# Sums for the first token pair of the second expert layer: temporaries in the row buffers instead of the relu buffers

## The chip, the cores and the metric

The kernel runs on one core of a Trainium2 chip. The metric is device microseconds of one execution. Before the change the median of 3 runs is 716.48 us (714.12 to 718.5).

## What is computed

Causal attention with a bias from a cumulated gate, then a layer in which each of 1152 tokens goes to one of 8 experts, then a layer in which each token goes through all 4 experts with weights of its own:

```python
attn_out = _attn_ref(**attn_kwargs)                      # B, H, S, D = 2, 8, 576, 64
x = attn_out.transpose(0, 2, 1, 3).reshape(B * S, H * D) # 1152 x 512
x = _moe_ref(x=x, **moe_kwargs)    # out[mask] = gate_w * (relu(x[mask] @ w1[e]) @ w2[e]), one of 8
return _moe2_ref(x=x, **moe2_kwargs)  # out += p[:, e] * (relu(x @ w1[e]) @ w2[e]), all 4; F = 1024
```

## The kernel before

**Attention** and the routing come first; the change is behind them.

**The first expert layer** runs over 8 slots, one expert each, with fixed capacities `CAPS` (128 to 248 columns; slot 7 has 188). For a slot, `fetch` starts the loads of the gathered rows (`xw`, pool `mp`, tag "xw", two buffers of 128 x 2 x 512 f32) and of the weights, `turn_x` (L728 to L733) transposes the rows on TensorE into `xs`, `layer1` (L777 to L784) multiplies by the first weight in eight groups `f` = 0 to 7 into PSUM tiles `pg` (three buffers) and evicts each through relu into `hb`, even groups by ScalarE (L784), odd ones by VectorE (L782). `layer2` (L804) multiplies `hb` by the second weight in four column blocks `dc`, and `put_y` (L790, L792) evicts them into `xf`. The tile `hb` has the tag "hh" and a single buffer, so a slot's `hb` may be written only when the tile that had the buffer before is read for the last time. The tag "hl" belongs to a lower part that only the split slot (248 columns) has. The transposes of slot 7's rows stand ahead of slot 6's `layer2`.

**Between slots 6 and 7** the program calls `build(0, ...)`: it prepares the moving operands of the second layer for the first pair of token blocks (2 x 288 columns of `xf`). The second layer multiplies 2 x 2 blocks with seven products in place of eight, so `build` makes four sums of blocks (`tsum`, two tiles of 128 x 2 x 2 x 288 f32, each with two sums; L648 on VectorE), and for every block and sum a rounded high part (`xbh`, `xth`; ScalarE, L645 and L649) and a low part (`xbl`, `xtl`; VectorE, L646 and L650). Its sums 1 and 3 are formed from sum 0, sum 1 in the first temporary and sum 3 in the second. The two temporaries take tiles of the tags named in the call.

**Beside it** the first weights of the second layer are prepared: four sums (`wsum`, L865 to L868) and, by `finish_first`, high parts (`hi`, ScalarE L872) and low parts (`wl`, VectorE L873) of 128 x 1024. The two weight tiles of `second_half` are loaded (L656) when buffers of the pool `wp` come free, and summed by GpSimd (L903). Slot 7's own weights are loaded ahead of these.

**After slot 7** stands `tc.If(most > 0)` (L914), a branch that handles tokens above the capacities; no instruction of its body runs with these inputs. All engines pass through the branch. Then the second layer starts with `first_layer` (L958) and keeps TensorE busy to the end.

A scheduler orders each engine's instructions from this program text, buffers and estimated times, so that the rows of one engine can be in another order than the calls.

Of the kernel before, what the change touches and what calls it, by code (L numbers as in the profile page):

```python
# [381 lines left out]
def tile_attention_moe_moe(  # L382
# [210 lines left out]
    mp = top1.enter_context(tc.tile_pool(name="mp", bufs=1))  # L593
# [38 lines left out]
    def build(c, pool, tags, bufs=1):  # L632

        o = 2 * HT * c
        blk = lambda j, k: xf[:, 2 * j : 2 * j + 2, o + k * HT : o + (k + 1) * HT]
        if ops[c] is None:
            ops[c] = [(pool if c else xo).tile([P, n, 2, HT], F32R, name=f"x{w}{c}") for w, n in (("bh", 3), ("bl", 3), ("th", 4), ("tl", 4))]
        bh, bl, th, tl = ops[c]
        t = [pool.tile([P, 2, 2, HT], F32, tag=tag, name="tsum", bufs=bufs) for tag in tags]
        base = (blk(0, 0), blk(1, 0), blk(1, 1))  # L640
        one, two = t[0][:, 0], t[0][:, 1]
        sums = ((0, one, blk(0, 1), blk(0, 0)), (2, t[1][:, 0], blk(1, 1), blk(0, 1)), (1, two, blk(1, 1), one), (3, t[1][:, 1], blk(1, 0), two))
        for i in range(4):
            if i < 3:
                nc.scalar.activation(out=bh[:, i], in_=base[i], func=AF.Copy)  # L645
                nc.vector.tensor_tensor(out=bl[:, i], in0=base[i], in1=bh[:, i].bitcast(F32), op=ALU.subtract)  # L646
            j, o_, x, y = sums[i]
            nc.vector.tensor_tensor(out=o_, in0=x, in1=y, op=ALU.subtract)  # L648
            nc.scalar.activation(out=th[:, j], in_=o_, func=AF.Copy)  # L649
            nc.vector.tensor_tensor(out=tl[:, j], in0=o_, in1=th[:, j].bitcast(F32), op=ALU.subtract)  # L650
# [22 lines left out]
    def reg(ap, engines, hi):  # L673
        return nc.values_load(ap, engines=engines, min_val=0, max_val=hi, skip_runtime_bounds_check_because="by construction")
# [43 lines left out]
    def turn_x(xw, cap, split):  # L718

        xs = mp.tile([P, KC, 256], F32R if split else F32, tag="xs", name="xs", bufs=2)  # L720
        xsl = mp.tile([P, KC, 256], F32R, tag="xs", name="xsl", bufs=2) if split else None
        for j in range(2):
            pt = ps.tile([P, 2, 256], F32, tag="tp", name="tp")
            for jj in range(2):
                for i in range(-(-cap // P)):
                    w = min(P, cap - i * P)
                    cc = 2 * j + jj
                    nc.tensor.transpose(out=pt[:, jj, i * P : i * P + w], in_=xw[:w, i, cc * P : (cc + 1) * P], identity=ident[:w, :w])  # L728
            o = xs[:, 2 * j : 2 * j + 2, :cap]
            if j == 0 or split:  # L730
                nc.scalar.activation(out=o, in_=pt[:, :, :cap], func=AF.Copy)
            else:
                nc.vector.tensor_copy(out=o, in_=pt[:, :, :cap])  # L733
            if split:
                nc.vector.tensor_tensor(out=xsl[:, 2 * j : 2 * j + 2, :cap], in0=pt[:, :, :cap], in1=o.bitcast(F32), op=ALU.subtract)
        return xs, xsl
# [23 lines left out]
    def layer1(pa, xs, cap, load=None):  # L760
        xs, xsl = xs
        split = xsl is not None
        hb = mp.tile([P, FC, max(CAPS)], F32R if split else F32, tag="hh", name="hb")
        hbl = mp.tile([P, FC, max(CAPS)], F32R, tag="hl", name="hbl") if split else None
        marks[2] = hb
        for f in range(FC):
            if load and f % 2 == 0:
                load(f // 2)
            pg = ps.tile([P, 512], F32, tag="g1", name="pg", bufs=3)
            fs = slice((f % 2) * P, (f % 2) * P + P)  # L770
            w = pa[f // 2]
            pairs = ((w[0], xs), (w[0], xsl), (w[1], xs)) if split else ((w, xs),)
            n = len(pairs) * KC
            for i in range(n):
                wt, xt = pairs[i % len(pairs)]
                cc = i // len(pairs)
                nc.tensor.matmul(out=pg[:, :cap], lhsT=wt[:, cc, fs], rhs=xt[:, cc, :cap], start=i == 0, stop=i == n - 1)  # L777
            if split:
                nc.scalar.activation(out=hb[:, f, :cap], in_=pg[:, :cap], func=AF.Relu)
                marks[0] = nc.vector.scalar_tensor_tensor(out=hbl[:, f, :cap], in0=pg[:, :cap], scalar=0.0, in1=hb[:, f, :cap].bitcast(F32), op0=ALU.max, op1=ALU.subtract)  # L780
            elif f % 2:
                marks[0] = nc.vector.tensor_scalar(out=hb[:, f, :cap], in0=pg[:, :cap], scalar1=0.0, scalar2=None, op0=ALU.max)  # L782
            else:
                nc.scalar.activation(out=hb[:, f, :cap], in_=pg[:, :cap], func=AF.Relu)  # L784
        return hb, hbl
# [23 lines left out]
    def fetch(sl):  # L809
        ev = reg(meta[0:1, 0, sl : sl + 1] if sl else e0[0:1, :], (ET.SP,), E1 - 1)  # L810
        rows = lambda a, w: region[ds(ev, 1), a : a + w, :].rearrange("o n d -> (o n) d")
        xw = [load_x(rows, CAPS[sl])] if sl else []
        first = None if sl else lambda: xw.append(load_x(rows, CAPS[sl]))
        pa, pb = load_w(w1[ds(ev, 1)].rearrange("o k f -> (o k) f"), w2[ds(ev, 1)].rearrange("o k f -> (o k) f"), SPLIT[sl], first, True)
        if sl == 0:
            put_rows(L0, L0 + LATE)
        return pa, pb, xw[0]

    r0 = reg(e0[0:1, :], (ET.SP,), E1 - 1)
    pa, pb, xw = fetch(0)  # L820
# [13 lines left out]
    def later(pb, j):  # L834
        if j >= 2:
            with tc.issue_after(marks[0].ins):
                pb[j] = split_w(pb[j], home(4 + j))
# [6 lines left out]
    for sl in range(E1):  # L844
        last = sl == E1 - 1
        hs = layer1(pa, xs, CAPS[sl], rest if sl == 0 else (lambda j: later(pb, j)) if SPLIT[sl] else None)
        if sl == 0:
            with tc.issue_after(marks[0].ins):
                gates()
        if not last:  # L850
            na, nb_, xw = fetch(sl + 1)
            xs = turn_x(xw, CAPS[sl + 1], SPLIT[sl + 1])
        if sl == 1:
            most = reg(meta[0:1, 4, 0:1], everyone, N)
        off = reg(meta[0:1, 2, sl : sl + 1], (ET.Activation, ET.DVE), N if sl > 3 else sl * N // E1)
        layer2(pb, hs, off, CAPS[sl])
        if not last:
            pa, pb = na, nb_
        if sl == E1 - 2:

            build(0, mp, ("hl", "hh"))

    def four_sums(g, a, eng):

# [49 lines left out]
    with tc.If(most > 0):  # L914
        with tc.For_i(0, E1, 1) as sl:
            ev = reg(meta[0:1, 0, ds(sl, 1)], (ET.SP,), E1 - 1)
            cnt_r = reg(meta[0:1, 1, ds(sl, 1)], (ET.SP, ET.Activation, ET.DVE), N)
            off_r = reg(meta[0:1, 2, ds(sl, 1)], (ET.Activation, ET.DVE), N)
            ov_r = reg(meta[0:1, 3, ds(sl, 1)], everyone, N)
            with tc.For_i(0, ov_r, P) as i:  # L920
                within = lambda x, hi: nc.s_assert_within(x, 0, hi, skip_runtime_bounds_check_because="i < count - capacity")
                r0 = within(cnt_r - P - i, N - P)
                ox = load_x(lambda a, w: region[ds(ev, 1), ds(r0, w), :].rearrange("o n d -> (o n) d"), P)
                xt = turn_x(ox, P, False)
                wt = mp.tile([P, 3, 4 * 256], F32, tag="hl", name="wt")
                part = lambda j, c: wt[:, j % 3, :].rearrange("p (c f) -> p c f", c=c)
                ht = layer1([part(j, KC) for j in range(4)], xt, P, lambda j: load_a(part(j, KC), w1[ds(ev, 1)].rearrange("o k f -> (o k) f"), j))
                oo = within(off_r + cnt_r - P - i, N - P)
                for dc in range(KC):
                    py = ps.tile([P, 512], F32, tag="g2", name="py", bufs=3)  # L930
                    wc = wt[:, dc % 3, :].rearrange("p (c d) -> p c d", c=FC)
                    nc.sync.dma_start(out=wc, in_=w2[ds(ev, 1), :, dc * P : (dc + 1) * P].rearrange("o (c p) d -> p (o c) d", p=P))
                    for f in range(FC):
                        nc.tensor.matmul(out=py[:, :P], lhsT=wc[:, f, :], rhs=ht[0][:, f, :P], start=f == 0, stop=f == FC - 1)
                    put_y(dc, py[:, :P], oo, P)
        build(0, mp, ("hl", "hh"))
    top1.close()


# [176 lines left out]
```

## Time and profile before

| | |
|---|---|
| runs | 714.12, 716.48, 718.5 us |
| profiled execution | 723.46 us, of it the span 721.8 us |
| mean granted TensorE clock, share of full speed | 0.971 |
| busy | TensorE 95%, VectorE 62%, ScalarE 46%, GpSimd 23% |

All durations below come from the profiled execution, which is 7.0 us above the median of the runs. An engine's instructions run in order; what stands in brackets behind a row of the timeline is the idle time of that engine ahead of the row, and what ended it. A share of busy time is a mean over stages with different limits, so the stage around the change is read by itself, by its time line, its waits and its clock.

### The profile page before, as it was taken

To read this page: it belongs to the slowest core of one execution; us is meant where nothing else is said; L and a number is where in the kernel's file an instruction comes from. 1 tells how busy PE (TensorE), PEld (TensorE's weight loads), DVE (VectorE), ACT (ScalarE), POOL (GpSimd) and SP (SyncE) were. 2 spreads that over 40 slices of the span, in tenths; PEclk is the share of its full clock that TensorE was granted. 3 is DMA by queue.
4 is the path that set the end of the run, shared out by engine and by line. 5 is a ranking of instruction groups with operands and counts; after the bars stand their busy time and mean duration, and the time that the engine had idled before them with its cause. 6 is when DMAs were issued, how large, how long until landed. Compare 5 with 4: busy or idle time off the path is not lost.

```text
span 721.8 us, 12757 instructions
## 1 busy us (share of the span) xinstructions
PE 688.4 (95%) x4829; PEld 638.9 (89%) x4830; DVE 444.4 (62%) x1006; ACT 332.3 (46%) x617; POOL 167.6 (23%) x193
## 2 busy tenths in 40 slices
PE   7899999979899999968999999999999999999996
PEld 5799999868799999968999989989899899998995
DVE  7586867662017111453787775877869668777583
ACT  5576767521116111332652836636437265383541
POOL 2000000033300000001053423632336124332333
PEclk9899999979899999989999999999999999999998
DMA  6746666029986977310011110111011101211002
GB/s 139 190 111 181 156 178 176 1 109 340 364 273 208 330 245 233 113 59 3 1 60 59 59 56 5 59 59 45 16 57 59 59 1 59 60 59 39 21 30 102
DMA packets 87015, 78.92 MB, mean 109 GB/s; under 512 B 42699, under 2 KB 67275, under 8 KB 86951
## 3 DMA queue, kind: packets, MB, share of 16 engines
q1 hardware_dynamic: 83063, 72.76, 33.2%
q0 software_dynamic: 1776, 4.79, 1.8%
q10 hardware_dynamic: 2112, 0.52, 0.4%
q8 instruction: 39, 0.64, 0.4%
q14 instruction: 25, 0.20, 0.1%
HBM read 69.08 MB, written 8.99 MB: 108 GB/s over the span
## 4 chain that ended last, share of the span: by engine, by line
PE 49%; issue 1%; DVE 1%; ACT 1%; POOL 0%; POOLq 0%
PE py L1049 15%; PE qa L958 14%; PE qd L958 7%; PE qa L1036 6%; PE qb L958 4%; PE qd L1036 3%; PE qb L1036 1%; DVE acc L1009 1%; ACT hr L981 0%; POOL out_dram L403 0%; ACT hi L872 0%; POOLq L1111 0%; ACT hr L975 0%; DVE sl L873 0%; POOLq L403 0%
## 5 line engine op out<-in xcount | busy, mean ns | idle before, releaser
L975 ACT ACTIVATE hr<-qa 128x288 f32<-128x288 f32 x96 | 37.3, 407 | 93.5 <-PE qa L958 93.5
L903 POOL TENSOR_TENSOR wsum<-w 128x512 f32<-128x512 f32 x16 | 24.3, 1532 | 238.6 <-PE pg L777 128.7
L777 PE MATMUL pg<-xs,w 128*128 128x128 f32 (+6 forms) x448 | 66.9, 313 | 9.4 <-ACT hb L784 6.1
L777 PEld LDWEIGHTS pg<-xs,w 128*128 128x128 f32 x448 | 65.3, 205 | 10.5 <-ACT hb L784 6.4
L872 ACT ACTIVATE bh<-hr 128x512 fp32r<-128x512 f32 (+1 forms) x72 | 41.1, 584 | 62.8 <-PE py L1049 57.5
L1049 PE MATMUL py<-hi,bl 128*128 128x512 f32 x160 | 63.0, 394 | 0.0
L1049 PE MATMUL py<-hi,bh 128*128 128x512 f32 x160 | 63.0, 394 | 0.0
L1049 PE MATMUL py<-wl,bh 128*128 128x512 f32 x160 | 63.0, 394 | 0.0
L804 PE MATMUL py<-hb,w 128*128 128x128 f32 (+6 forms) x448 | 61.9, 296 | 0.7 <-DMA w<-in_moe_w_dram 0.7
L804 PEld LDWEIGHTS py<-hb,w 128*128 128x128 f32 x448 | 59.5, 190 | 1.5 <-DMA w<-in_moe_w_dram 1.1
L873 DVE TENSOR_TENSOR bl<-hr,bh 128x512 fp32r<-128x512 f32 (+1 forms) x72 | 55.5, 779 | 3.1 <-ACT bh L872 2.8
L283 PE MATMUL av<-vt,ptT 128*128 128x65 f32 x320 | 47.1, 279 | 0.0
L873 DVE TENSOR_TENSOR wl<-w,hi 128x1024 fp32r<-128x1024 f32 x32 | 45.4, 1420 | 0.0
L258 ACT ACTIVATE p<-p,mn 128x512 f32<-128x512 f32 (+4 forms) x72 | 40.6, 582 | 10.1 <-DVE mn L246 9.5
L1009 DVE SCALAR_TENSOR_TENSOR acc<-py,aux,acc 128x512 f32<-128x512 f32 x35 | 26.3, 751 | 28.4 <-PE py L1049 28.4
L271 ACT ACTIVATE ptT<-pt 128x512 f32<-128x512 f32 (+3 forms) x80 | 34.3, 434 | 19.3 <-PE pt L269 19.0
L283 PEld LDWEIGHTS av<-vt,ptT 128*128 128x128 f32 x320 | 42.5, 197 | 0.3
L958 PE MATMUL qa<-xbh,hi 128*128 128x288 f32 x128 | 39.6, 309 | 2.7 <-DVEq L914 2.6
L872 ACT ACTIVATE hi<-wsum 128x1024 fp32r<-128x1024 f32 x32 | 33.0, 1057 | 16.1 <-POOL wsum L868 13.3
L873 DVE TENSOR_TENSOR wl<-wsum,hi 128x1024 fp32r<-128x1024 f32 x32 | 38.9, 1216 | 0.0
L246 DVE CUSTOM_DVE_ANT_0 p<-sc,p 128x512 f32<-128x512 f32 (+4 forms) x72 | 34.6, 484 | 7.0 <-PE sc L209 4.3
L782 DVE TENSOR_SCALAR hb<-pg 128x128 f32<-128x128 f32 (+6 forms) x28 | 8.9, 317 | 48.5 <-PE pg L777 48.4
(297 smaller groups left out, 2044.8 us busy)
## 6 DMA issues: line engine op xcount, KB each, us to landing
w<-in_moe_w_dram SPq DMA_DIRECT2D x96, 512.0 KB
region<-zrow SPq DMA_DIRECT2D x8, 512.0 KB
bc<-ncum_d SPq DMA_DIRECT2D x7, 576.0 KB
ks<-in_k_dram SPq DMA_DIRECT2D x28, 128.0 KB
br<-ncum_d SPq DMA_DIRECT2D x16, 144.0 KB
qs<-in_q_dram SPq DMA_DIRECT2D x16, 128.0 KB
vt<-in_v_dram SPq DMA_DIRECT2D x16, 128.0 KB
xw<-region SPq DMA_DIRECT2D x8, 256.0 KB
```

The source lines that it names most:

```text
L246: self.last[1] = nc.vector.tensor_tensor_reduce(out=t[:, lo : lo + w], in0=st["sc"][:, 0:w], in1=t[:, lo : lo + w], scale=1.0, scalar=init ...
L258: self.last[0] = nc.scalar.activation(out=t[:, 0:w], in_=t[:, 0:w], func=AF.Exp, scale=-1.0, bias=st["mn"][:, 0:1])
L271: nc.scalar.activation(out=pt[:r, : n * P], in_=ps[:r, : n * P], func=AF.Copy)
L283: nc.tensor.matmul(out=av[b][:, 65 * c : 65 * c + 65], lhsT=st[("pt", j)], rhs=d["vt"][:, j, b, :], start=j == 0, stop=j == c)
L777: nc.tensor.matmul(out=pg[:, :cap], lhsT=wt[:, cc, fs], rhs=xt[:, cc, :cap], start=i == 0, stop=i == n - 1)
L804: nc.tensor.matmul(out=py[:, :cap], lhsT=wt[:, f % 2, dcs], rhs=ht[:, f, :cap], start=f == 0 and i == 0, stop=f == FC - 1 and i == len(pai ...
L872: nc.scalar.activation(out=hi, in_=t, func=AF.Copy)
L873: nc.vector.tensor_tensor(out=lo, in0=t, in1=hi.bitcast(F32), op=ALU.subtract)
L958: nc.tensor.matmul(out=out[:, :HT], lhsT=a, rhs=b, start=start and n == 0, stop=n == 5, skip_group_check=True)
L975: nc.scalar.activation(out=o, in_=y, func=AF.Copy)
L1036: nc.tensor.matmul(out=q, lhsT=x[:, k, :], rhs=y[:, k, :], start=m == 0 and name not in ACCUMULATED, stop=m == 5, skip_group_check=True)
L1049: nc.tensor.matmul(out=py, lhsT=x[:, f, :], rhs=y[:, f % 2, :], start=f == i == 0, stop=f == 3 and i == 2)
```

## The change

`build(0, ...)` takes its two temporaries from the tag "xw", which has two buffers, instead of one from "hl" and one from "hh". The first call is the one between slots 6 and 7, the second stands in the branch that does not run. The buffers of "xw" grow from 4096 to 4608 bytes per partition, since a temporary has 2 x 2 x 288 f32. No instruction of the computation is added or removed.

```diff
@@ -858,7 +858,7 @@
         if sl == E1 - 2:
 
-            build(0, mp, ("hl", "hh"))
+            build(0, mp, ("xw", "xw"), 2)
@@ -933,7 +933,7 @@
                     put_y(dc, py[:, :P], oo, P)
-        build(0, mp, ("hl", "hh"))
+        build(0, mp, ("xw", "xw"), 2)
     top1.close()
```

The scheduler answers with another order on two engines; TensorE, GpSimd and SyncE keep theirs. VectorE (DVE) during slot 7's `layer1`, from the third sum of `build` on (`hb<-pg` are the evictions of slot 7's odd groups, `wl` the low parts of the second layer's weights):

```order
 L650 TENSOR_TENSOR xtl_3622<-tsum,xth_3621 128x576
 L648 TENSOR_TENSOR tsum<-xf,tsum 128x576
-L873 TENSOR_TENSOR wl<-wsum,hi 128x1024
+L782 TENSOR_SCALAR hb<-pg 128x188
+L648 TENSOR_TENSOR tsum<-xf,tsum 128x576
 L650 TENSOR_TENSOR xtl_3622<-tsum,xth_3621 128x576
-L648 TENSOR_TENSOR tsum<-xf,tsum 128x576
-L873 TENSOR_TENSOR wl<-w,hi 128x1024
+L782 TENSOR_SCALAR hb<-pg 128x188
 L650 TENSOR_TENSOR xtl_3622<-tsum,xth_3621 128x576
 L873 TENSOR_TENSOR wl<-wsum,hi 128x1024
-L782 TENSOR_SCALAR hb<-pg 128x188 x4
+L782 TENSOR_SCALAR hb<-pg 128x188
+L873 TENSOR_TENSOR wl<-w,hi 128x1024
+L873 TENSOR_TENSOR wl<-wsum,hi 128x1024
+L782 TENSOR_SCALAR hb<-pg 128x188
```

The four evictions, which stood behind all of `build` and behind all low parts, now stand between them: one after the third sum, one after the third low part of the sums, one ahead of the last two low parts of the weights, one at the end.

ScalarE (ACT) in the same place (`hb<-pg` are the even groups, `hi<-w` x2 the high parts of the two tiles that L656 loads):

```order
 L645 ACTIVATE xbh_3619<-xf 128x576 x2
-L649 ACTIVATE xth_3621<-tsum 128x576 x3
+L649 ACTIVATE xth_3621<-tsum 128x576
 L784 ACTIVATE hb<-pg 128x188 x2
+L649 ACTIVATE xth_3621<-tsum 128x576 x2
+L784 ACTIVATE hb<-pg 128x188 x2
+L674 TENSOR_LOAD meta
+L792 ISA
+L792 ACTIVATE xf<-py 128x188
 L872 ACTIVATE hi<-w 128x1024 x2
-L784 ACTIVATE hb<-pg 128x188 x2
-L674 TENSOR_LOAD meta
-L792 ISA
-L792 ACTIVATE xf<-py 128x188
```

The first two evictions move ahead of the last two high parts of the sums, and the two high parts of the loaded weights move behind `layer1`, behind the first eviction of slot 7's `layer2`.

## Rows read from the trace of the kernel before

**Rows 1.** The page: span, busy time, and the groups of the chain that ended last.

```profile
span 721.8 us, 12757 instructions
PE 688.4 (95%) x4829; PEld 638.9 (89%) x4830; DVE 444.4 (62%) x1006; ACT 332.3 (46%) x617; POOL 167.6 (23%) x193
PE 49%; issue 1%; DVE 1%; ACT 1%; POOL 0%; POOLq 0%
```

**Rows 2.** Timeline of TensorE around slot 7: start us, us, what, [idle before, releaser].

```profile
294.58 1.85 PE L728 MATMUL tp<-ident,xw 128*128 128x128 f32 x8
296.37 9.60 PE L804 MATMUL py<-hb,w 128*128 128x172 f32 x64
305.80 3.98 PE L777 MATMUL pg<-xs,w 128*128 128x188 f32 x24
315.87 9.65 PE L777 MATMUL pg<-xs,w 128*128 128x188 f32 x40 [6.08 <-ACT hb L784]
325.35 10.35 PE L804 MATMUL py<-hb,w 128*128 128x188 f32 x64
338.28 0.37 PE L958 MATMUL qa<-xbh,hi 128*128 128x288 f32 x1 [2.58 <-DVEq L914]
```

**Rows 3.** Windows: stretch, then us, busy by engine (PE, PEld, DVE, ACT, POOL), PEclk, DMA, GB/s.

```profile
309.80:313.00 3.20, 0.00 (x0) 0.00 (x0) 3.20 (x5) 0.68 (x1) 0.00 (x0) 1.00 0.00 0
313.00:315.90 2.90, 0.04 (x1) 0.04 (x1) 2.90 (x4) 1.10 (x3) 0.00 (x0) 0.88 0.00 0
315.90:322.00 6.10, 6.10 (x20) 6.10 (x21) 1.24 (x3) 1.44 (x3) 0.00 (x0) 0.50 0.52 175
322.00:325.40 3.40, 3.40 (x23) 3.40 (x23) 0.35 (x1) 1.35 (x3) 2.27 (x2) 1.00 0.00 0
339.00:342.40 3.40, 3.40 (x17) 3.40 (x16) 3.39 (x5) 2.52 (x5) 0.00 (x0) 0.51 0.00 0
```

**Rows 4.** Timeline of ScalarE from `build`'s second part to slot 7's evictions.

```profile
307.39 1.24 ACT L645 ACTIVATE xbh<-xf 128x576 fp32r<-128x576 f32 x2
308.54 0.67 ACT L649 ACTIVATE xth<-tsum 128x576 fp32r<-128x576 f32 x1
313.62 0.68 ACT L649 ACTIVATE xth<-tsum 128x576 fp32r<-128x576 f32 x1 [1.79 <-DVE tsum L648]
315.48 0.55 ACT L784 ACTIVATE hb<-pg 128x188 f32<-128x188 f32 x2 [1.18 <-DVE xtl L650]
318.48 1.06 ACT L872 ACTIVATE hi<-w 128x1024 fp32r<-128x1024 f32 x1 [2.45 <-DMA w<-in_moe_w_dram]
321.75 1.06 ACT L872 ACTIVATE hi<-w 128x1024 fp32r<-128x1024 f32 x1 [2.21 <-SPq L914]
```

**Rows 5.** Timeline of VectorE in the same stretch.

```profile
301.78 0.76 DVE L648 TENSOR_TENSOR tsum<-xf 128x576 f32<-128x576 f32 x1
...
306.56 1.21 DVE L873 TENSOR_TENSOR wl<-w,hi 128x1024 fp32r<-128x1024 f32 x1
307.69 0.75 DVE L648 TENSOR_TENSOR tsum<-xf 128x576 f32<-128x576 f32 x1
308.36 1.42 DVE L646 TENSOR_TENSOR xbl<-xf,xbh 128x576 fp32r<-128x576 f32 x2
309.70 0.75 DVE L650 TENSOR_TENSOR xtl<-tsum,xth 128x576 fp32r<-128x576 f32 x1
310.37 0.75 DVE L648 TENSOR_TENSOR tsum<-xf,tsum 128x576 f32<-128x576 f32 x1
...
314.64 0.75 DVE L650 TENSOR_TENSOR xtl<-tsum,xth 128x576 fp32r<-128x576 f32 x1
315.31 1.22 DVE L873 TENSOR_TENSOR wl<-wsum,hi 128x1024 fp32r<-128x1024 f32 x1
316.45 0.34 DVE L782 TENSOR_SCALAR hb<-pg 128x188 f32<-128x188 f32 x1
```

**Rows 6.** Timeline of the DMA issues of SyncE, stretch 300 to 345 us.

```profile
314.80 2.56 SPq L656 DMA_DIRECT2D w<-in_moe_w_dram  x2
```

**Rows 7.** Timeline of VectorE and GpSimd at the end of slot 7.

```profile
323.06 1.27 POOL L903 TENSOR_TENSOR wsum<-w 128x512 f32<-128x512 f32 x1 [128.70 <-PE pg L777]
335.73 1.26 POOL L903 TENSOR_TENSOR wsum<-w,wsum 128x512 f32<-128x512 f32 x1
335.74 0.35 DVE L790 COPY xf<-py 128x188 f32 x1 [4.74 <-PE py L804]
336.01 2.07 DVE L873 TENSOR_TENSOR wl<-w,hi 128x1024 fp32r<-128x1024 f32 x1
```

## The prediction

> **What bounds the kernel now.** Over the whole span TensorE is the bound: 688.4 us of 721.8 us busy, and the chain that ended last runs mostly through it [rows 1]. So the change can only be worth what TensorE loses where slot 7 of the first expert layer waits. I read that stage in this order: TensorE's timeline, then its clock, then the engines that it waited for.
>
> TensorE's timeline [rows 2] shows the one hole. Slot 7's `layer1` has 64 matmul records, eight for each group. After 24, that is three groups, as many as there are `pg` buffers, it stands for 6.08 us, until ScalarE has evicted into `hb`. Nothing else in these rows waits: 294.58 to 309.78 us and 315.87 to 335.70 us are without a gap.
>
> The clock [rows 3] shows what the hole costs beyond itself. During the hole the granted clock falls (1.00 in its first part, 0.88 as the mean of 313.0 to 315.9 us), and from 315.90 to 322.00 us the matmuls run at 0.50, the lower of the two levels, 1.2 GHz; from 322.00 us on it is 2.4 GHz again.
>
> ScalarE and VectorE show why `hb` was late. ScalarE's first eviction starts at 315.48 us, and was released by an `xtl` on VectorE [rows 4]. That is the last of `build`'s low parts, 314.64 us plus 0.75 us [rows 5]: it is the last reader of the temporary that had the buffer of tag "hh", the same single buffer that slot 7's `hb` needs. The PSUM tile itself had been ready since 307 us (305.80 us and eight records). VectorE had no idle time from 306.56 us to that point; it did `build` and the low parts of the weights one after the other.
>
> **The change part by part.** It removes one dependency: `hb` of slot 7 after the last read of `build`'s second temporary. It adds another: the temporaries after the last read of the row tiles of slots 6 and 7. The later of these reads are the transposes that start at 294.58 us and are over at 296.43 us [rows 2]; the first sum starts at 301.78 us and the second temporary at 307.69 us [rows 5]. The added wait costs nothing, with 5.4 us to spare. The loads of these rows came before their transposes, so a wait on them is over too.
>
> *The hole.* 6.08 us of TensorE's idle time go if the evictions come in time in the new order. I lay the new order out with the spacings of the old rows. TensorE: a record of 188 columns at the full clock takes 10.35 / 64 = 0.162 us [rows 2], a group 1.29 us, so the groups end at 307.1, 308.4, 309.7, 311.0, 312.3, 313.6, 314.9 and 316.2 us. ScalarE: the first three operand parts end at 309.21 us [rows 4], so group 0 is out at about 309.5 us, and group 3 wants its buffer at 309.7 us. VectorE [rows 5], by starts of consecutive rows: an operation of 128 x 576 takes 0.67 us, one of 128 x 1024 1.13 us, an eviction 0.34 us at most. The third sum starts at 310.37 us, group 1 is evicted from 311.04 to 311.38 us, then the fourth sum and an `xtl` (312.72 us), group 3 to 313.06 us, `xtl` and `wl` (314.87 us), group 5 to 315.2 us, two `wl` (317.5 us), group 7 to 317.8 us. Group 4 would want group 1's buffer at 311.0 us: 0.4 us late if it takes that one, not late if it takes group 2's, which ScalarE evicts at about 310.0 us. Group 6 wants group 3's buffer at 313.6 us, which is out at 313.06 us. `layer2` starts at 316.2 us and wants group 7 with its fifteenth record, at 318.4 us; it is out at 317.8 us. So a new wait is between 0 and 0.4 us; I take 0.2 us, the middle, since the margins are of the size of the spacings' rounding.
>
> *The clock.* The 40 records after the hole take 325.35 - 315.87 = 9.48 us; at the full clock they would take 40 x 0.162 = 6.48 us. These 3.0 us go as well if the clock doesn't fall, and it fell here only after TensorE had stood for over 3 us [rows 3]; a wait of 0.4 us is far from that. Lower bound of this term: 0, if something else makes the clock fall. Sum so far: 6.08 + 3.0 - 0.2 = **8.9 us**, with which `layer2` of slot 7 ends at 326.8 us instead of 335.70 us.
>
> *What is late next.* The second layer starts at 338.28 us, after a gap of 2.58 us that ends with VectorE's branch [rows 2]. VectorE gets there after the last eviction of slot 7 (335.74 us) and a `wl` of 2.07 us [rows 7]; both follow `layer2`, and stay behind it in the new order. So the gap moves along, unless that `wl` has to wait for its weights. Their loads don't move forward with TensorE: they were issued from 314.80 us on [rows 6], as the low parts of the weights set buffers free, and the last of those now ends at 317.5 us in place of 316.5 us. The second loaded tile was worked on by ScalarE at 321.75 us [rows 4], 7.0 us after the first issue. At the latest it is then 317.5 + 7.0 + 1.06 = 325.6 us, against 326.8 us when VectorE wants it: 1.2 us to spare even so. The two high parts, which now stand ahead of the third eviction of `layer2` on ScalarE, are covered too: that eviction is due at 316.2 + 3 x 2.59 = 324.0 us, at worst it comes 1.6 us late, and only the fourth column block, which has the first one's PSUM buffer or a free one, is still on TensorE then. Cost of both: 0, with a bound of 1.6 us.
>
> GpSimd's sums (L903) start at 323.06 us, when slot 7's weights set a buffer free [rows 7]; they may start some us earlier, as early as the loads land. There a rule speaks against the change. What the row shows first: the `wl` at 336.01 us took 2.07 us, with a GpSimd sum running from 335.73 us on, where the same shape took 1.21 us at 306.56 us without one [rows 5, 7]. The Trainium skill (SBUF — State Buffer, section SBUF: two separate sides) says that a VectorE `tensor_tensor` with both inputs in SBUF and a GpSimd operation exclude each other from a shared port pair for the whole instruction; the trace agrees, as far as these two rows go, and by that rule a GpSimd sum that starts early would hold up the two `wl` ahead of group 7's eviction. In rows: 2.07 - 1.21 = 0.86 us, against a margin of 0.6 us (317.8 to 318.4 us), so 0.3 us; but the first load was used 3.7 us after its issue (314.80 to 318.48 us) [rows 4, 6], its buffer comes free no earlier than before, and so it lands after 317.8 us. The collision is not to be expected.
>
> From 338.28 us on nothing changes but the time at which it starts. The fall of the clock from 339.00 to 342.40 us, behind the second gap [rows 3], costs half of 3.4 us, 1.7 us; it may come at another moment after that gap, or not at all, which is a possible further gain of up to 1.7 us.
>
> The sum is made against the profiled execution: 723.46 - 8.9 = 714.6 us there. Its runs' median is 7.0 us lower, and I take the gain in us over unchanged: 716.48 - 8.9 = **707.6 us**.
>
> **The rivals.**
>
> *The hole goes, but the time comes back in small waits or a slow clock.* For it: the margins above are 0.2 to 0.6 us, VectorE is without idle time until 317.8 us, and the estimates carry every error forward. If VectorE runs 1 us late throughout, groups 4 and 6 and `layer2` wait about 1 us each in turn, not in sum, since they wait for the same engine: 1 to 2 us. If moreover the clock falls, its 3.0 us stay. Gain 8.9 - 2 - 3 = 4 us to 7 us, so 709.5 to 712.5 us. Against it: the `layer2` of slots 6 and 7, with evictions that alternate between both engines, show no gap [rows 2].
>
> *Nothing to be had.* Either the buffers of "xw" are not free (a later user that I overlooked) or the second layer's start is held by the loads. The spare times above (5.4 us and 1.2 us) speak against both. Time 716.5 us.
>
> *Slower.* One mechanism: VectorE's pace leaves TensorE with so many short waits that the granted clock falls early in slot 7's `layer1` and stays at 1.2 GHz to the end of `layer2`. If it holds for the last 40 records of `layer1` and the 64 of `layer2`, these take 104 x 0.162 = 16.8 us more than at the full clock, so the result is 16.8 - 9.1 = 7.7 us worse, 724 us. It decides in this direction from 56 records at half speed on (9.1 / 0.162). Against it: in the trace the clock came back while 20 records ran at half speed without a gap, within 6.1 us [rows 3], and the waits laid out above are one of 0.4 us at most.
>
> **How the numbers follow.** My forecast (gain of 7 us or more) has a chance of 0.80, the partial gain 0.12, nothing 0.05, slower 0.03. The predicted time is that of the forecast. The lower end of the range is 8.9 us of gain, 1.7 us for the second fall of the clock and 1.9 us for the spread of the runs (they lie up to 2.4 us from their median): 704.0 us. The upper end takes in the partial gain but for its last us: 711.5 us. A measurement of this kernel can tell some 0.5%, 3.6 us, from no change. All of the forecast and nearly all of the partial gain lie beyond it: faster 0.91, same 0.06, slower 0.03.
>
> **What would show it.** Right: no wait of `pg` for `hb` of over 0.5 us in slot 7's `layer1`; its 64 records in one piece of some 10.4 us; PEclk at 1.00 from 305 to 326 us; the second layer's first matmul some 9 us earlier, still behind VectorE's branch with a gap of about 2.6 us; everything behind it as long as before, but for the clock. Wrong: a hole in `layer1` that ends with an eviction on VectorE (then the order of its work decides), a clock of 0.50 without a hole, or a longer gap ahead of L958 with ScalarE waiting for a load (then the loads, which do not move forward, are the new limit).

## The result and the profile after

The change runs in 708.75 us (median of 4 runs, 706.25 to 710.58), the kernel before in 717.49 us (4 runs, one more than stood above): 8.7 us less by medians. The ratio, which is taken from all runs of both kernels and not from the two medians, is 0.9883 with a 95% interval of 0.9833 to 0.9932, that is 5 to 12 us. The forecast was 8.9 us. Two more measurements of the same pair, each on another occasion, gave ratios of 0.9896 (0.9867 to 0.9926) and 0.9849 (0.982 to 0.9878).

TensorE's timeline after the change, the answer to [rows 2]:

```profile
289.67 1.85 PE L728 MATMUL tp<-ident,xw 128*128 128x128 f32 x8
291.45 9.60 PE L804 MATMUL py<-hb,w 128*128 128x172 f32 x64
300.89 10.35 PE L777 MATMUL pg<-xs,w 128*128 128x188 f32 x64
311.07 10.35 PE L804 MATMUL py<-hb,w 128*128 128x188 f32 x64
324.00 0.37 PE L958 MATMUL qa<-xbh,hi 128*128 128x288 f32 x1 [2.58 <-DVEq L914]
```

The 64 records of slot 7's `layer1`, which stood in two rows with 6.08 us between them, are one row. From the start of `layer1` to the start of `layer2` it was 325.35 - 305.80 = 19.55 us and is 311.07 - 300.89 = 10.18 us: 9.37 us less. From there to the first matmul of the second layer it was 12.93 us and is 12.93 us, with the same gap of 2.58 us at the same branch. The whole stage, `layer1` to second layer, went from 32.48 to 23.11 us.

The windows of the same stretch, the answer to [rows 3] (stretch, us, busy by engine, then PEclk, DMA, GB/s):

```profile
300.89:311.07 10.18, 10.18 (x66) 10.18 (x65) 10.15 (x17) 5.22 (x10) 0.00 (x0) 1.00 0.00 1
311.07:321.30 10.23, 10.23 (x66) 10.06 (x64) 1.93 (x4) 2.65 (x4) 3.62 (x3) 1.00 0.34 105
321.42:324.00 2.58, 0.00 (x1) 0.03 (x1) 2.34 (x2) 0.00 (x0) 1.30 (x2) 1.00 0.03 10
324.00:328.50 4.50, 4.50 (x34) 4.50 (x35) 3.77 (x5) 3.35 (x7) 0.00 (x0) 1.00 0.00 0
```

The clock is at 2.4 GHz throughout, and this time it did not fall behind the second gap either. VectorE is busy for 10.15 of 10.18 us, and TensorE no longer waits for it.

VectorE in `layer1` after the change, the answer to [rows 5]; the evictions are the rows `hb<-pg`:

```profile
305.45 0.75 DVE L648 TENSOR_TENSOR tsum<-xf,tsum 128x576 f32<-128x576 f32 x1
306.12 0.34 DVE L782 TENSOR_SCALAR hb<-pg 128x188 f32<-128x188 f32 x1
306.38 0.74 DVE L648 TENSOR_TENSOR tsum<-xf,tsum 128x576 f32<-128x576 f32 x1
307.04 0.75 DVE L650 TENSOR_TENSOR xtl<-tsum,xth 128x576 fp32r<-128x576 f32 x1
307.71 0.34 DVE L782 TENSOR_SCALAR hb<-pg 128x188 f32<-128x188 f32 x1
...
309.78 0.34 DVE L782 TENSOR_SCALAR hb<-pg 128x188 f32<-128x188 f32 x1
...
312.31 0.34 DVE L782 TENSOR_SCALAR hb<-pg 128x188 f32<-128x188 f32 x1
```

The profiled executions differ by more than the runs: spans of 721.8 and 708.0 us, 13.8 us apart. Of these, 9.37 us lie in slot 7; 4.91 us lie ahead of it (305.80 against 300.89 us), and 0.5 us was lost behind it. The part ahead is not the change's. The windows from 160 to 240 us, first before, then after, show a stretch in which the DMA engines are busy for 90 and 98% of the time, and which ran at other rates, 300 and 320 GB/s (the last column):

```profile
160.00:240.00 80.00, 74.08 (x562) 70.82 (x563) 24.30 (x65) 18.63 (x42) 14.18 (x14) 0.93 0.90 300
```

```profile
160.00:240.00 80.00, 74.91 (x604) 72.43 (x605) 25.61 (x78) 18.98 (x43) 14.21 (x14) 0.97 0.98 320
```

A kernel with the same order of instructions as the change (the first experiment) reaches slot 7's `layer1` at 305.75 us in its profile, with 294 GB/s in that stretch, while a kernel with the order of before (the second run of the filled hole) reaches it at 300.11 us. Over all fourteen profiles it begins between 297.1 and 309.0 us. So lengths from the start of `layer1` on are compared below, not points in time. From there to the end of TensorE's last matmul it was 410.2 us and is 401.1 us, 9.1 us less.

### The profile page after: what moved, and what is told of

Its sections match the earlier page's. It is cut to its first block, busy times and chain, and to the rows that moved or that the text cites. A ratio compares the mean times of both kernels' runs of the same rounds, so it can differ in the third digit from the quotient of the medians.

```text
span 708.0 us, 12759 instructions
## 1 busy us (share of the span) xinstructions
PE 682.5 (96%) x4829; PEld 632.5 (89%) x4830; DVE 444.8 (63%) x1006; ACT 332.1 (47%) x617; POOL 166.8 (24%) x193
## 3 DMA queue, kind: packets, MB, share of 16 engines
q0 software_dynamic: 1776, 4.79, 1.8%
## 4 chain that ended last, share of the span: by engine, by line
PE 51%; issue 1%; DVE 1%; ACT 1%; POOL 0%; POOLq 0%
PE py L1049 15%; PE qa L958 14%; PE qd L958 7%; PE qa L1036 6%; PE qb L958 4%; PE qd L1036 3%; PE qb L1036 1%; DVE acc L1009 1%; ACT hr L981 0%; POOL out_dram L403 0%; ACT hi L872 0%; POOLq L1111 0%; ACT hr L975 0%; DVE acc L1007 0%; DVE sl L873 0%
## 5 line engine op out<-in xcount | busy, mean ns | idle before, releaser
L1049 PE MATMUL py<-hi,bl 128*128 128x512 f32 x160 | 63.0, 394 | 0.0
L1049 PE MATMUL py<-hi,bh 128*128 128x512 f32 x160 | 63.0, 394 | 0.0
L1049 PE MATMUL py<-wl,bh 128*128 128x512 f32 x160 | 63.0, 394 | 0.0
L777 PE MATMUL pg<-xs,w 128*128 128x128 f32 (+6 forms) x448 | 59.9, 294 | 0.2 <-ACT xs L753 0.2
L777 PEld LDWEIGHTS pg<-xs,w 128*128 128x128 f32 x448 | 59.0, 190 | 0.3 <-ACT xs L753 0.3
L958 PE MATMUL qa<-xbh,hi 128*128 128x288 f32 x128 | 39.3, 307 | 2.7 <-DVEq L914 2.6
L958 PE MATMUL qa<-xth,hi 128*128 128x288 f32 x128 | 37.9, 296 | 0.2 <-ACT hr L975 0.2
```

The source lines that it names most:

```text
L958: nc.tensor.matmul(out=out[:, :HT], lhsT=a, rhs=b, start=start and n == 0, stop=n == 5, skip_group_check=True)
L1049: nc.tensor.matmul(out=py, lhsT=x[:, f, :], rhs=y[:, f % 2, :], start=f == i == 0, stop=f == 3 and i == 2)
```

## The experiments

**The second temporary alone.** The buffers were moved one at a time. `build` gives "xw" its two buffers, every other tag one.

```diff
-            build(0, mp, ("hl", "hh"))
+            build(0, mp, ("hl", "xw"))
```

> Only the second temporary moves (tag "hh" to "xw"); the first stays in "hl". Theory (slot 7's hb waited for the second temporary alone, because both had the one buffer of "hh"): the full gain, 8 to 9.5 us below before, no gap in the 64 records of slot 7's layer1, clock 1.00 there. Rival (the first temporary's place counts too, or the larger row buffers do): less than 6 us, or a gap left in layer1.

714.18 us against 722.9 us, ratio 0.9871 (0.9839 to 0.9903): the full gain. The order of every engine is the change's. In TensorE's timeline `layer1` has no gap, and from its start to TensorE's end it takes 402.2 us:

```profile
305.75 10.35 PE L777 MATMUL pg<-xs,w 128*128 128x188 f32 x64
315.94 10.35 PE L804 MATMUL py<-hb,w 128*128 128x188 f32 x64
```

**The first temporary alone.**

```diff
-            build(0, mp, ("hl", "hh"))
+            build(0, mp, ("xw", "hh"))
```

> Only the first temporary moves (tag "hl" to "xw"); the second stays in "hh". Theory: no gain (within 2 us of before), a gap of about 6.1 us after 24 records of slot 7's layer1 that ends with ScalarE's eviction, then about 6 us at a clock of 0.50. Rival (moving either temporary loosens the order): half of the gain or more.

722.41 us against 722.9 us, ratio 0.9991 (0.9971 to 1.0011): nothing, and in TensorE's timeline the hole is the old one:

```profile
306.69 3.98 PE L777 MATMUL pg<-xs,w 128*128 128x188 f32 x24
316.75 8.99 PE L777 MATMUL pg<-xs,w 128*128 128x188 f32 x40 [6.08 <-ACT hb L784]
325.58 10.35 PE L804 MATMUL py<-hb,w 128*128 128x188 f32 x64
```

Together the two show that the one buffer of "hh", shared by `build`'s second temporary and slot 7's `hb`, was the whole cause. The move out of "hl" does nothing for the time, and neither do the larger buffers of "xw", which both runs have.

**The hole filled.** This separates the hole from the clock: the kernel before, with matmuls in the hole that nobody reads.

```diff
+            if cap == CAPS[-1] and f == 3:
+                pd = ps.tile([P, 2, 256], F32, tag="tp", name="pd")
+                for i in range(26):
+                    nc.tensor.matmul(out=pd[:, 0, :P], lhsT=ident, rhs=ident, start=True, stop=True)
             pg = ps.tile([P, 512], F32, tag="g1", name="pg", bufs=3)
```

> The kernel before, with 26 matmuls of 128 columns between groups 2 and 3 of slot 7's layer1, into a PSUM tile that nobody reads: they fill the gap (some 5.7 us at the full clock) without changing who waits for whom. Theory (the gap cost twice, 6.1 us by itself and 3.0 us by the clock that fell in it): the other records of layer1 stay where the evictions let them be, but run at 1.00, so slot 7's layer2 begins about 3.0 us earlier than before, measured from the start of layer1: 16.5 us instead of 19.55 us; whole kernel 2 to 3.5 us faster than before. Rival (the 0.50 after the gap has another cause, such as the loads that land then): the clock falls all the same and the time is that of before or more.

TensorE's timeline of the first of two runs (L772 is the fill, whose 26 matmuls leave two records each; the lines behind it are four further down than in the kernel before), and below it the window of the records behind the fill, with PEclk, DMA and GB/s at the end:

```profile
309.00 3.98 PE L781 MATMUL pg<-xs,w 128*128 128x188 f32 x24
312.82 5.97 PE L772 MATMUL pd<-ident 128*128 128x128 f32 x52
319.07 6.63 PE L781 MATMUL pg<-xs,w 128*128 128x188 f32 x40 [0.28 <-ACT hb L788]
325.54 10.35 PE L808 MATMUL py<-hb,w 128*128 128x188 f32 x64
```

```profile
319.00:325.50 6.50, 6.43 (x40) 6.43 (x41) 1.70 (x4) 2.53 (x6) 2.18 (x2) 1.00 0.53 164
```

From `layer1` to `layer2` it takes 16.54 us, as the theory had it, and the 40 records behind the fill ran at 1.00, though the two loads landed beside them. So the half clock came from the hole and not from the loads. The run time moved less: 722.34 us against 722.9 us, 0.6 us by medians; the ratio of 0.9976 (0.9952 to 1.0) makes it 1.7 us. That is below the 2 us I expected at least, so it was run again.

> The kernel before with the 26 filling matmuls once more, since its first run gave 1.7 us with an interval from 0 to 3.5 us, while its stage was 16.5 us as expected. Theory (the clock term is 2.4 to 3.0 us, and the stretch ahead of slot 7 only scatters): the stage again 16.4 to 16.7 us, the kernel 1.5 to 3.5 us below before. Rival (the fill costs elsewhere what it saves in the stage): within 1 us of before.

The stage is 16.53 us (300.11 to 316.64 us) again; the time is 714.42 us against 717.62 us, 3.2 us by medians and 2.2 us by the ratio of 0.997 (0.9943 to 0.9998). Both runs together put the clock's share at about 2 us of run time, with intervals from 0 to 4 us; the 3.0 us of the stage lie within them and are neither confirmed nor refuted by run time. The half clock also does not cost the same in every execution: in the profile of the run with the first temporary alone, the 40 records took 325.58 - 316.75 = 8.83 us, not 9.48 us.

The two profiles of this one kernel show one thing more. These are the first 6 us of the second layer in the first and in the second of them, each behind the same gap of 2.58 us:

```profile
338.47:344.47 6.00, 6.00 (x45) 6.00 (x46) 5.24 (x7) 4.47 (x10) 0.00 (x0) 1.00 0.01 3
329.57:335.57 6.00, 6.00 (x34) 6.00 (x35) 5.24 (x7) 3.44 (x7) 0.00 (x0) 0.72 0.01 3
```

So the second fall of the clock comes in one execution and not in another of the same kernel.

**The buffers without the order.** The change, with slot 7's evictions queued behind the last high part (ScalarE) and the last low part (VectorE) of `build`.

```diff
-            nc.scalar.activation(out=th[:, j], in_=o_, func=AF.Copy)
-            nc.vector.tensor_tensor(out=tl[:, j], in0=o_, in1=th[:, j].bitcast(F32), op=ALU.subtract)
+            ends[0] = nc.scalar.activation(out=th[:, j], in_=o_, func=AF.Copy)
+            ends[1] = nc.vector.tensor_tensor(out=tl[:, j], in0=o_, in1=th[:, j].bitcast(F32), op=ALU.subtract)
...
+                with tc.issue_after(ends[f % 2].ins) if cap == CAPS[-1] else ExitStack():
```

> The change, but slot 7's evictions are queued behind the last operand part of build on their engine (ScalarE: the last high part, VectorE: the last low part), with the buffers of the change. Theory (the buffers give nothing by themselves, the gain is the order that they allow): the gap is back, some 4.5 to 5.5 us, since ScalarE's last high part ended 1.2 us ahead of the low part that released it before; the clock falls in it; the kernel is 0.5 to 3 us below before, 6 to 8.5 us above the change. Rival (the wait for the buffer itself was the cost, whatever the order): most of the 9 us stays.

723.56 us against 722.9 us, ratio 1.0 (0.9975 to 1.0025). TensorE's timeline:

```profile
306.31 3.98 PE L778 MATMUL pg<-xs,w 128*128 128x188 f32 x24
315.08 9.56 PE L778 MATMUL pg<-xs,w 128*128 128x188 f32 x40 [4.79 <-ACT hb L787]
324.48 10.35 PE L807 MATMUL py<-hb,w 128*128 128x188 f32 x64
```

The hole is 4.79 us, within the expected 4.5 to 5.5 us, with the clock at 0.50 behind it (314.31 to 320.31 us), and `layer1` to `layer2` takes 18.17 us, 1.4 us less than before. The run time does not show the gain of 0.5 us or more that I expected; its interval reaches 1.8 us to either side, so a gain of that size is not ruled out. The free buffer is worth little or nothing while the evictions are queued behind `build`: the gain is the order that the buffer permits.

**More work on VectorE.** The change once more as the neighbour:

> The change itself once more, as the neighbour of the next three on the same chip: 8 to 9.5 us below before, no gap in slot 7's layer1.

708.12 us against 716.04 us, a gain of 7.9 us by medians, just under the 8 us expected; no gap in `layer1` (298.57 to 308.76 us). Beside it, each of `build`'s sums computed twice:

```diff
             nc.vector.tensor_tensor(out=o_, in0=x, in1=y, op=ALU.subtract)
+            if c == 0:
+                nc.vector.tensor_tensor(out=o_, in0=x, in1=y, op=ALU.subtract)
```

> The change, with each of the four sums of build's first call computed twice (the same values): 4 x 0.67 = 2.7 us more work on VectorE, most of it ahead of slot 7's evictions. Theory (VectorE has some 0.5 to 1 us in hand at each eviction, and its low parts can go behind them): TensorE's gaps in slot 7's layer1 and layer2 stay under 1 us in sum, the clock stays at 1.00, the kernel is within 1.5 us of the change. Rival (VectorE sets the pace of that stage): the 2.7 us show up as gaps on TensorE in full, and more if the clock falls with them.

TensorE's timeline of this run:

```profile
300.15 10.35 PE L779 MATMUL pg<-xs,w 128*128 128x188 f32 x64
310.33 10.35 PE L806 MATMUL py<-hb,w 128*128 128x188 f32 x64
```

No gap, 10.18 us to `layer2`, 707.46 us: the same as the change within the runs. The scheduler put all four remaining `wl` behind the evictions of groups 1 to 5. So 2.7 us more of VectorE's work cost nothing, and the margins of 0.2 to 0.6 us that I had computed are not the limit for it: the low parts of the weights are work that can move back. The scheduler knew of this work and reordered for it. What VectorE costs when it runs later than planned this run does not show; a later one does.

**The gap ahead of the second layer.** The 2.58 us gap is VectorE's `wl`, which has to wait for a buffer of `wp` that slot 7's `layer2` reads to its end. With more of a slot's second-weight tiles in another pool, `wq`, a `wp` buffer is free earlier.

```diff
-    wq = top1.enter_context(tc.tile_pool(name="wq", bufs=8))
+    wq = top1.enter_context(tc.tile_pool(name="wq", bufs=10))
-    home = lambda i: wq if i in (1, 3, 4, 6) else wp
+    home = lambda i: wq if i in (1, 3, 4, 6, 7) else wp
```

> The change, with the last second-weight tile of each slot in the pool wq (10 buffers for 8), so that a buffer of wp is free for the last low part ahead of the second layer before slot 7's layer2 has ended. Theory (the 2.58 us gap ahead of the second layer's first matmul is VectorE's low part of 2.07 us behind the last eviction): the gap shrinks to 0.5 to 1.2 us, and the kernel is 1 to 3.5 us below the change. Rival (the branch itself or the start of the second layer holds TensorE as long, or the loads come at worse times from the new pools): gap or time unchanged.

And the same with `(1, 3, 4, 5, 6, 7)` and 12 buffers:

> As the one before, with the last three second-weight tiles in wq (12 buffers): both low parts are free to run ahead of slot 7's last eviction. Theory: the same gap of 0.5 to 1.2 us, the kernel 1 to 4 us below the change, unless VectorE then stands for a load ahead of that eviction; in that case a gap in slot 7's layer2 of up to 3 us gives it back. Rival as above.

707.36 us and 706.48 us beside the change's 708.12 us; against before 0.9887 (0.9856 to 0.9919) and 0.9867 (0.9834 to 0.9899), so neither can be told from the change, and only the second is 1 us or more below it by medians. TensorE's timeline of the second shows why:

```profile
299.10 6.53 PE L777 MATMUL pg<-xs,w 128*128 128x188 f32 x40
306.97 4.09 PE L777 MATMUL pg<-xs,w 128*128 128x188 f32 x24 [1.35 <-DVE hb L782]
310.89 10.35 PE L804 MATMUL py<-hb,w 128*128 128x188 f32 x64
323.02 0.37 PE L958 MATMUL qa<-xbh,hi 128*128 128x288 f32 x1 [1.78 <-PEq L914]
```

The gap ahead of the second layer shrank from 2.58 to 1.78 us and not to the 0.5 to 1.2 us expected: what is left is the last eviction and the branch. But a new gap of 1.35 us stands in `layer1`, and the stage is 23.92 us instead of 23.11 us; the first version has the same two gaps, 1.38 and 1.77 us. VectorE's timeline of this run, and below it GpSimd's, show what went with it:

```profile
301.74 0.75 DVE L650 TENSOR_TENSOR xtl<-tsum,xth 128x576 fp32r<-128x576 f32 x1
302.41 1.83 DVE L646 TENSOR_TENSOR xbl<-xf,xbh 128x576 fp32r<-128x576 f32 x1
304.16 1.82 DVE L650 TENSOR_TENSOR xtl<-tsum,xth 128x576 fp32r<-128x576 f32 x1
305.91 0.74 DVE L648 TENSOR_TENSOR tsum<-xf,tsum 128x576 f32<-128x576 f32 x1
306.57 0.60 DVE L782 TENSOR_SCALAR hb<-pg 128x188 f32<-128x188 f32 x2
```

```profile
301.89 1.73 POOL L903 TENSOR_TENSOR wsum<-w 128x512 f32<-128x512 f32 x1 [9.60 <-PE pg L777]
303.58 1.78 POOL L903 TENSOR_TENSOR wsum<-w,wsum 128x512 f32<-128x512 f32 x1
```

With loads and buffers early, GpSimd's sums start in `layer1`, and VectorE's operations take 1.83 us in place of 0.75 us while they run. Twice 1.08 us makes group 1's eviction late: without them it would start at 304.41 us, and TensorE came to want its buffer at 305.63 us. That the sums slow these operations is read from the rows; no run moves the sums alone.

**That eviction on ScalarE.** The change as the neighbour on this occasion, and both pool versions with one more line:

```diff
-            elif f % 2:
+            elif f % 2 and (cap != CAPS[-1] or f != 1):
```

> The change itself, as the neighbour of the next two on the same chip: 7.5 to 9.5 us below before.

> The last three second-weight tiles in wq (12 buffers), and slot 7's group 1 evicted by ScalarE instead of VectorE. In the run without this second part VectorE's eviction of group 1 came late, behind two operations of 128 x 576 that took 1.8 us instead of 0.75 us while GpSimd's sums ran, and TensorE stood for 1.35 us in layer1. Theory (that eviction alone set the gap): no gap over 0.4 us in layer1, the gap ahead of the second layer stays at about 1.8 us, the stage from the start of layer1 to the second layer's first matmul takes 22.3 to 22.8 us (23.1 us in the change, 23.9 us in the run without), the kernel 1.5 to 3.5 us below the change. Rival (groups 3 and 5, still on VectorE, take its place): a gap of about 1 us remains and the kernel is within 1.5 us of the change.

> The same with the last second-weight tile alone in wq (10 buffers). Theory: no gap over 0.4 us in layer1, the stage 22.3 to 22.8 us, the kernel 1 to 3 us below the change. Rival as above; besides, the high parts of the loaded weights stand between the evictions on ScalarE here, and a load that lands late would hold groups 4 and 6: a gap of 1 to 3 us in layer1.

The change 707.61 us, 9.9 us below before by medians and so a little more than expected, the two versions 704.42 us (703.73 to 706.82) and 704.8 us (703.2 to 707.44), against 717.54 us for before: ratios 0.9849 (0.982 to 0.9878), 0.9828 (0.9801 to 0.9854) and 0.9833 (0.9804 to 0.9863). TensorE in the first of them:

```profile
297.44 10.69 PE L777 MATMUL pg<-xs,w 128*128 128x188 f32 x64
307.96 10.35 PE L804 MATMUL py<-hb,w 128*128 128x188 f32 x64
320.22 0.37 PE L958 MATMUL qa<-xbh,hi 128*128 128x288 f32 x1 [1.91 <-PEq L914]
```

The new gap is gone but for 0.34 us (`layer1` to `layer2` 10.52 us), and the stage is 22.78 us and 22.68 us, as expected. By medians the two are 3.2 and 2.8 us below the change, of which the profiles show 0.3 to 0.4 us in the stage. Both low parts of the loaded weights now stand ahead of the second layer, where one of them stood in its beginning, and the second layer's first part, from L958 to the first matmul of L1049, takes 30.6 and 31.0 us against 31.4 to 31.6 us in the change's three profiles. The intervals overlap with the change's, so they are the fastest here by medians, and not surely faster than the change.

## Why the prediction was right

- **The wait.** `hb` of slot 7 waited for the last reader of `build`'s second temporary: shown by the pair of runs that moved one temporary each. The prediction had named the second temporary, by its buffer of tag "hh"; the first had no part.
- **The hole, 6.08 us.** It went in full. The new wait, put at 0 to 0.4 us and taken as 0.2 us, was 0: that term was too large by its whole size. VectorE's evictions ended at 306.46, 308.05, 310.12 and 312.65 us; counted from the start of `layer1`, that is 5.6, 7.2, 9.2 and 11.8 us against 5.6, 7.3, 9.4 and 12.0 us in the layout from the old rows. The chain was good to 0.2 us.
- **The clock, 3.0 us.** The half clock went with the hole, and the run with the filled hole shows that the hole made it fall. The size was read from one execution; the stage confirms it (16.54 and 16.53 us against 19.55 us), while run time gave about 2 us, with intervals from 0 to 4 us.
- **The sum.** 9.37 us in the profiled stage and 7.9, 8.7 and 9.9 us by medians of the three measurements, against 8.9 us. The mechanism is what was forecast; that the first measurement lies within 0.2 us of it is chance, with an interval of 5 to 12 us. The stage exceeds the forecast by 0.5 us: 0.2 us is the wait that did not come, and 0.3 us comes from the 0.162 us per record, which divides a row that ends with its last record's end; from start to start it is 10.18 / 64 = 0.159 us. From the start of `layer1` to TensorE's end, the three profiles with the hole of before or most of it (the kernel before, the first temporary alone, the held order) take 410.2, 410.3 and 410.6 us, the three of the change 401.1, 400.4 and 400.4 us.
- **What comes next.** The loads did not move forward against `layer1`: issued 9.0 us after its start before [rows 2, 6], 9.05 us after (309.94 us). The second loaded tile was worked on at 316.69 us and wanted at 321.73 us; the 1.2 us to spare of the worst case were 4 us. GpSimd's first sum started at 313.76 us, behind group 7's eviction at 312.31 us, so the collision ahead of that eviction did not come; the old one ahead of the second layer, a `wl` of 2.07 us, stayed. GpSimd's sums were the right thing to fear: when a later edit brought them forward, they met VectorE's work ahead of an eviction, and TensorE stood for 1.35 us.
- **The second fall of the clock.** It was absent in the profile after, and the first matmul of L1049 comes 31.5 us behind the start of the second layer instead of 32.6 us. It is absent in the change's two other profiles too, but the order in slot 7 alone does not decide it: the fall came in the run with the second temporary alone, which has the change's order (PEclk 0.74 in the first 6 us of the second layer), and in one of the two profiles of the filled hole. From the first matmul of L1049 to the last it took 346.1 us instead of 344.7 us, so nothing of it shows at the end. That stretch, counted to the end of the last matmul, takes 344.5 to 346.5 us over the fourteen profiles, in no relation to the order in slot 7; what makes it vary is open.
- **The base.** The prediction set the gain against a profiled execution 7 us above the runs and carried it over in us. The result fits that, and the profiles say why it could: what differs most between executions is the time ahead of slot 7, 297.1 to 309.0 us, where the change does nothing, while the part behind it is the same to 0.4 us in the three profiles named above. That the 7 us of the one execution lie there fits these numbers but is not shown, since no execution of the kernel before near 716 us was profiled.

## What to carry to other kernels

A tile of one buffer that a side task borrows between two uses of the main loop can make the main loop wait for the side task's last read, as here, with the PSUM tiles ready 8 us earlier; look for a third tile that is already dead there, and then see that the scheduler uses the freedom, since with the old order held the free buffer gave no measurable time. A TensorE gap of some us costs more than itself where the profile shows the clock at half behind it. Freeing buffers also lets other engines' work start earlier: look at what they share before counting on the rest of the gain.

## What the runs showed of the hardware

VectorE's subtraction of two 128 x 576 f32 operands took 1.83 and 1.82 us while GpSimd's sums of 128 x 512 ran, 0.75 us otherwise, and those sums took 1.73 and 1.78 us instead of 1.27 us (the run with 12 buffers). The Trainium skill (SBUF — State Buffer, section SBUF: two separate sides) says that such a pair excludes each other from one port pair for a whole instruction; these rows agree with it, in both directions: each of VectorE's two ends 0.62 us behind the end of a GpSimd sum (304.24 against 303.62 us, 305.98 against 305.36 us), about the 0.67 us from start to start of an undisturbed one. VectorE's work out of PSUM beside GpSimd's sums kept its times: a copy at 335.74 us in the kernel before took 0.35 us, and an eviction at 306.81 us in the last version with 10 buffers 0.34 us.

In the hole of the kernel before, which lasted from 309.78 to 315.87 us, the granted clock (third number from the end, read here for half a microsecond at a time) fell only late. With the hole filled, and 0.28 us of idle time behind the filling, it stayed at 1.00.

```profile
314.50:315.00 0.50, 0.00 (x0) 0.00 (x0) 0.50 (x2) 0.00 (x0) 0.00 (x0) 1.00 0.00 0
315.00:315.50 0.50, 0.00 (x0) 0.00 (x0) 0.50 (x2) 0.02 (x1) 0.00 (x0) 0.70 0.00 0
315.50:316.00 0.50, 0.14 (x1) 0.14 (x1) 0.50 (x1) 0.50 (x2) 0.00 (x0) 0.50 0.00 0
```
